# State matrices in column halves where the neighbours run in column halves, and an order of work grouped by the tiling of the TensorE array

## Chip, cores, metric

One core of one Trainium2 chip. The metric is the device time in microseconds of one execution. Several executions of each kernel were timed; one of each run was also profiled, and its span (first to last instruction) is about 2 us (1.7 to 2.3 in the record) shorter than its timed value. Some executions show a lower granted TensorE clock (down to 0.983 in the record), or are over 1.5% above the fastest of their kernel; the record calls them slow. Medians below are of all executions, ratios of fast ones alone. The experiments ran in four sittings, on chips 10, 14, 1 and 12, each beside the kernel before in the same rounds. In the profiles PE is TensorE, PEld its weight loads, DVE VectorE, ACT ScalarE, POOL GpSimd, SP SyncE; a "q" behind a name is the engine's instruction queue.

## The reference, cut to what matters

```python
# A: a diagonal state-space layer, 640 complex states, 2048 steps, 640 channels
Lam_bar = jnp.exp(dt * Lam)
h = Lam_bar[None, :] * h + Bu[:, t, :]                 # for t in range(2048)
y = 2.0 * jnp.einsum("blp,dp->bld", hseq, Cmat).real + x * Dskip
# B: shifted k times v, a long convolution over 2048 steps by FFT, times q
y = irfft(rfft(kv, 4096) * rfft(ssm_k, 4096))[:2048] + kv * ssm_D
out = jnp.concatenate([a, q * y], axis=-1)             # 2048 x 1280, bfloat16
```

## The kernel before

The kernel computes A by blocks: projections into the states, powers of the state matrices (`M[n]`, 128x128) that carry a state over n steps, and an output projection. B is a transform in two stages forward (s1, s2) and two back (i2, i1). All of it is one graph of 722 operations; a text, `ORDER`, gives the order of emission, the engine and the buffer slot of each. What matters here is how the matmuls lie in the array; the sizes are those that the profile prints for the weights, 128*128 for the whole array:

```python
# dn (L630): 128 rows x 64 columns, two halves of the columns side by side
nc.tensor.matmul(P[64 * ri:64 * ri + 64, b, :], lhsT=self.BT[:, k, ri, 64 * j:64 * j + 64], rhs=self.xT[...])
# m1 (L638): the whole array
for r, n in ((2, 1), (1, 2), (0, 3)):
    nc.tensor.matmul(self.P(pt)[:, 1, 256:512], lhsT=M[n][:, j, :],
                     rhs=self.hb[:, j, hf, 256 * r:256 * r + 256], start=False, stop=True, skip_group_check=True)
# d0 (L731): the whole array, 512 columns; d1 (L715), S (L659), jw and jv (L677): the whole array
nc.tensor.matmul(self.P(p2)[:, 0, :]..., lhsT=M[1][:, j, :], rhs=src, start=True, stop=True)
# py (L778, L782): output projection and skip term, the whole array
nc.tensor.matmul(P[:, part, 0:320], lhsT=hap(j), rhs=self.CT[:, j, c0:c0 + 320], start=(j == 0), stop=False)
# s1 (L881): 64x64.  s2 (L917): 128x64.  i2 (L973): 64x128.  i1 (L1009): 128x64.  ct (L758): 64x128
...
ORDER = """
...
x131 dn1_4_0 e1_2_0/D e1_1_0/A set_4_0/G hst0/S@2 set_8_0/D m1_2_0 e3_0_0/A x100 m1_1_0 ct@3 dn0_9_0@6 ...
"""
```

Every `e...` is a copy out of PSUM (L209 on ScalarE, L211 on VectorE).

## Time and profile before

| | before |
|---|---|
| timed, median of 4 (range) | 211.53 us (210.95 to 213.7) |
| span of the profiled execution (itself timed at 213.1) | 210.9 us |
| TensorE busy | 194.0 us, 92% |
| VectorE, ScalarE busy | 169.3, 148.1 us |
| waits of TensorE that the profile lists | 12.8 us, 5.1 of them before its first matmul |

A reader should not stop at "92% busy". The ends of matmuls are modelled, so time lost between two matmuls can lie under the busy row (ten L630 that start at 54.84 last 1.25 us by the profile, and the next matmul starts 1.18 us after 54.84); the starts in the order of time show it. The prediction below quotes those lines. Its 111 and 98 ns are the mean durations of weight loads, and its 3 to 4 ns the time between the starts of the two matmuls of a pair.

### The profile page before, as it was taken

How to read it: one execution, taken by the hardware profiler on the slowest of the kernel's cores; microseconds unless marked ns; L12 is line 12 of the kernel's file. 1: busy time of each engine (PE TensorE's matmuls, PEld its weight loads, DVE VectorE, ACT ScalarE, POOL GpSimd, SP SyncE). 2: the span in 40 equal slices, each digit the busy share in tenths (PEclk: the TensorE clock that was granted, in tenths of full speed). 3: DMA queues.
4: the chain of work that ended last, by engine and by line, in shares of the span. 5: the costliest groups of instructions: out<-in, count | busy, mean ns of one | idle time of the engine just before them, and what ended most of it. 6: DMA issues, size and time to landing. Idle time of an engine off the chain costs nothing.

```text
span 210.9 us, 8671 instructions
## 1 busy us (share of the span) xinstructions
PE 194.0 (92%) x3947; PEld 132.6 (63%) x3947; DVE 169.3 (80%) x262; ACT 148.1 (70%) x174; POOL 28.4 (13%) x39
## 2 busy tenths in 40 slices
PE   0899999899998999997899999999999998999772
...
DVE  7899999958999697888679889888798798775540
...
GB/s 170 286 140 166 168 179 193 203 188 175 161 235 172 246 233 221 119 160 164 244 136 3 31 168 229 131 36 135 209 125 33 117 220 133 37 184 187 193 137 131
DMA packets 103094, 33.72 MB, mean 160 GB/s; under 512 B 99538, under 2 KB 101330, under 8 KB 103058
## 3 DMA queue, kind: packets, MB, share of 16 engines
...
q10 hardware_dynamic: 30, 0.00, 0.0%
HBM read 9.19 MB, written 7.86 MB: 81 GB/s over the span
## 4 chain that ended last, share of the span: by engine, by line
PE 60%; DMA 18%; DVE 12%; issue 5%; ACT 4%; POOL 0%; POOLq 0%; ACTq 0%; DVEq 0%
PE ps L778 19%; DMA s<-kvd 8%; PE ps L630 8%; PE ps L881 8%; PE ps L917 7%; DMA kvd<-s 5%; DMA s<-s 5%; PE ps L731 4%; PE ps L973 3%; PE ps L1009 3%; DVE s L940 3%; PE ps L782 2%; PE ps L715 2%; PE ps L638 1%; PE ps L758 1%
## 5 line engine op out<-in xcount | busy, mean ns | idle before, releaser
L209 ACT CAST s<-ps 128x1024 bf16<-128x1024 f32 x90 | 88.1, 1017 | 26.4 <-PE ps L881 10.3
L630 PE MATMUL ps<-xT,BC 128*64 128x512 bf16 x400 | 49.2, 386 | 0.2 <-ACT s L209 0.2
L778 PE MATMUL ps<-BC,hb 128*128 128x320 bf16 x240 | 36.6, 300 | 0.0
L630 PEld LDWEIGHTS <-BC 128*64 128x64 bf16 x400 | 21.3, 111 | 17.6 <-issue 2.4
L778 PEld LDWEIGHTS <-hb 128*128 128x128 bf16 x240 | 21.9, 98 | 9.5
L881 PE MATMUL ps<-R,s 64*64 64x128 bf16 x1280 | 23.9, 218 | 3.7 <-DMA s<-kvd 2.0
L940 DVE TENSOR_TENSOR s<-s,s 128x2048 bf16<-128x2048 bf16 x20 | 24.5, 1223 | 2.2 <-ACT s L209 1.5
L881 PEld LDWEIGHTS <-s 64*64 64x64 bf16 x1280 | 18.9, 106 | 10.1 <-issue 5.4
L735 DVE TENSOR_TENSOR hb<-ps,hb 128x512 bf16<-128x512 f32 x30 | 19.5, 685 | 5.2 <-PE ps L731 5.2
L209 ACT CAST yo<-ps 128x640 bf16<-128x640 f32 x10 | 6.9, 691 | 22.1 <-PE ps L782 21.5
L917 PE MATMUL ps<-s,Wre 128*64 128x128 bf16 x320 | 21.5, 222 | 0.0
L917 PE MATMUL ps<-s,Wim 128*64 128x128 bf16 x320 | 21.0, 219 | 0.0
L917 PEld LDWEIGHTS <-Wre 128*64 128x64 bf16 x320 | 17.4, 109 | 3.5 <-issue 1.3
L856 DVE TENSOR_TENSOR s<-s,s 128x2048 bf16<-128x2048 bf16 x15 | 18.5, 1237 | 0.8 <-ACT s L848 0.5
L917 PEld LDWEIGHTS <-Wim 128*64 128x64 bf16 x320 | 17.9, 110 | 0.8
L1016 DVE TENSOR_TENSOR s<-ps,s 128x1024 bf16<-128x1024 f32 x10 | 12.0, 1216 | 7.1 <-PE ps L1009 4.6
L211 DVE CAST s<-ps 128x1024 bf16<-128x1024 f32 x10 | 12.2, 1222 | 4.2 <-PE ps L973 1.8
L940 DVE TENSOR_TENSOR s<-s 128x1024 bf16<-128x1024 bf16 x20 | 13.7, 687 | 0.3
L1009 PE MATMUL ps<-Ct,s 128*64 128x64 bf16 x640 | 11.8, 196 | 1.8 <-DMA s<-s 1.8
L1009 PEld LDWEIGHTS <-s 128*64 128x64 bf16 x640 | 10.9, 113 | 3.3 <-DMA s<-s 2.0
L850 DVE TENSOR_SCALAR s<-s,sk 128x2048 bf16<-128x2048 bf16 x15 | 12.0, 808 | 0.3
L778 PE MATMUL ps<-BC,Qb 128*128 128x320 bf16 x80 | 12.2, 300 | 0.0
...
## 6 DMA issues: line engine op xcount, KB each, us to landing
...
```

What stands on the lines that cost most here:

```text
L209: self.nc.scalar.copy(out=out, in_=in_)
L211: self.eng[e].tensor_copy(out=out, in_=in_)
L630: nc.tensor.matmul(P[64 * ri:64 * ri + 64, b, :], lhsT=self.BT[:, k, ri, 64 * j:64 * j + 64], rhs=self.xT[:, k, hf, 2 * b:2 * b + 2, :].re ...
L735: v.tensor_tensor(out=hv(r), in0=self.P(p2)[:, 0, :].rearrange("p (h m) -> p h m", h=2), in1=hv(r), op=ALU.add)
L778: nc.tensor.matmul(P[:, part, 0:320], lhsT=hap(j), rhs=self.CT[:, j, c0:c0 + 320], start=(j == 0), stop=False)
L850: v.tensor_scalar_mul(out=out, in0=k(j), scalar1=self.sk[:, G, j:j + 1])
L856: op(f"ca{j}{G}{h}", {"DVE": dve_tt(W_)}, lambda e, c=c, tt=tt: v.tensor_tensor(out=c(), in0=c(), in1=tt(), op=ALU.add), r=[f"tm{G}{h}"], ...
L881: nc.tensor.matmul(P[64 * ri:64 * ri + 64, r, 128 * b4:128 * b4 + 128], lhsT=d[64 * r:64 * r + 64, 4 * qd + b4, a0, :], rhs=self.R[64 * r: ...
L917: nc.tensor.matmul(P[64 * pi:64 * pi + 64, ri, 128 * k4:128 * k4 + 128], lhsT=W[:, kp, pi, :], rhs=A[:, kp + 16 * pi, :], start=True, stop ...
L940: v.tensor_tensor(out=o, in0=a, in1=b, op=op_)
L1009: nc.tensor.matmul(P[64 * ah:64 * ah + 64, b // 8, 64 * (b % 8):64 * (b % 8) + 64], lhsT=Z[:, 16 * h + b, 64 * ri:64 * ri + 64], rhs=self. ...
L1016: v.tensor_tensor(out=o, in0=self.P(pt)[:].rearrange("p s (b a c) -> p a (s b) c", b=8, a=16), in1=o, op=ALU.mult)
```

## The change

Intent: TensorE loses time each time the tiling of the array changes, 0.10 us on leaving a block in the trace of before (called a drain below; it is a name for the measured loss, what the array does in it is not shown). So a whole-array matmul with a state matrix is emitted as two matmuls with 64 columns each where its neighbour that cannot choose runs in column halves; and the order is a new one in which work of one tiling stands together.

```diff
+FREE = ("m1_", "d0", "d1_", "S", "jw", "jv")
...
+    def split(self):
+        pe = [o for o in self.order if o.eng == "PE"]
+        before = None
+        for i, o in enumerate(pe):
+            if o.name.startswith(FREE):
+                if before is None:
+                    before = next((self.halves(q) for q in pe[i:] if not q.name.startswith(FREE)), None) or False
+                o.split = before
+            else:
+                before = self.halves(o)
+
+    def halves(self, o):
+        return True if o.name.startswith(("dn", "s2", "i1")) else False if o.name.startswith(("py", "px")) else None
...
+    def mm(self, o, out, lhsT, rhs, **k):
+        if self.g.by_name[o].split:
+            for h in (slice(0, 64), slice(64, 128)):
+                self.nc.tensor.matmul(out[h], lhsT=lhsT[:, h], rhs=rhs, **k)
+        else:
+            self.nc.tensor.matmul(out, lhsT=lhsT, rhs=rhs, **k)
...
-                nc.tensor.matmul(self.P(pt)[:, 1, 256:512], lhsT=M[n][:, j, :], ...
+                self.mm(f"m1_{u}", self.P(pt)[:, 1, 256:512], lhsT=M[n][:, j, :], ...
...                                   (the same for d0, d1, S, jw, jv)
 ORDER = """
-... (722 words, the old order)
+... (722 words, a new order; some copies and loads move to another engine or slot)
 """
```

(Cut: the helper's bookkeeping, cost figures that only label operations, and both orders.)

More of the change, by code (lines that the diff above doesn't have):

```diff
@@ L37 @@
     __slots__ = ("idx", "name", "alts", "fn", "deps", "succ", "bufs", "dma", "due", "own_due", "start", "end", "eng",
-                 "takes", "lat", "turn", "port")
+                 "takes", "lat", "turn", "port", "split")
 class Graph:
@@ L52, in __init__ @@
         self.order = []
+        self.by_name = {}
     def buf(self, tag, name, n=2):
@@ L59, in op @@
         o.idx, o.name, o.alts, o.fn, o.dma, o.own_due, o.turn = len(self.ops), name, alts, fn, dma, due, turn
-        o.lat, o.port = 2.0 if turn else 1.2, port
+        o.lat, o.port, o.split = 2.0 if turn else 1.2, port, False
         o.deps, o.succ, o.takes = set(), [], []
@@ L82, in op @@
         self.ops.append(o)
+        self.by_name[name] = o
         return o
@@ L87, in place @@
         letter = {"P": "PE", "A": "ACT", "D": "DVE", "G": "POOL", "S": "SP"}
-        ops = {o.name: o for o in self.ops}
+        ops = self.by_name
         done = set()
@@ L101, in place @@
         assert len(done) == len(self.ops)
+        self.split()
         return self.order
+    def split(self):
[10 more added lines that the diff above has]
+        return True if o.name.startswith(("dn", "s2", "i1")) else False if o.name.startswith(("py", "px")) else None
 def mm_cost(n, count=1):
@@ L126 @@
 ORDER = """
-ld_lre Dm0 w0 xn0@0 scol pidx B00 consts zero w1 J0 E0 kz1/G@0 kz0/G@1 wi0@2 w2 J1 ci0@1 ld_lim ld_ldt wi1@3 xn1@2 px00@0 bc
-B01 px02@1 ex00/A nrow wm1 kz2/G@4 c4 ex02/A par@2 px04@3 p0 wm0 dtb x130 px12@0 E1 ex04/A B10 nrowf px10@1 ex12/A px14@4 p1
-nrho fi rn mk ph x110 ci1 dn0_0_0@6 Dm1/S trig dn0_1_0@2 ex10/D ld_sk/S B11 ws0@5 ex14/D dn0_2_0@0 rc ss dn0_4_0@4 set_1_0/D
-set_2_1/G k0 dn1_0_0 set_2_0/D ws1@6 set_3_0/G dn1_1_0 x120 dn1_2_0 e1_0_0/D set_1_1/G m1_0_0 x131 dn1_4_0 e1_2_0/D e1_1_0/A
@@ L131 @@
-set_4_0/G hst0/S@2 set_8_0/D m1_2_0 e3_0_0/A x100 m1_1_0 ct@3 dn0_9_0@6 e3_1_0/D set_12_1/G dn0_8_0@2 sk e1_4_0/D dn1_9_0 R
-set_12_0/G v0@5 dn1_8_0 e1_9_0/A set_3_1/D m1_4_0 e3_2_0/A dn1_3_0@0 e3_4_0/A cs200/D@3 x111 e1_8_0/A dtap0/D m1_9_0 cv300/D@6
-s1h03@4,4 x121 e3_9_0/A ca200 m1_8_0 e1h03/A s1h00@6 dn0_3_0 x101 cs100/D e1h00/A ca100 s1h02@4 k1 e3_8_0/A s1h01@6 e1h02/A
-dn0_7_0@2 cs000/D e1h01/A den dn1_7_0 hst1/S@2 ca000 e1_3_0/A s2h01@4,5 m1_3_0 e2h01/A cm00 dn1_0_1@6 e1_7_0/A set_4_1/D
@@ L135 @@
-s2h03@4 kvs0/S cn10@0 dn0_0_1 e3_3_0/A g e2h03/A s2h02@0 dn0_4_1@4 e2h02/A dtap1/G m1_7_0 set_G_1/D set_8_1/G s1h11@0,2
-e3_7_0/A s1h13@2 e1h11/A dn1_4_1 e1_0_1/D set_G_0/G e1h13/A m1_0_1 s1h12@0 cs210/D@1 e1_4_1/A s1h10@2 e3_0_1/A cv310/D@3
-kvl0/S@5 v1@6 e1h12/A dn0_1_1@6 ca210 e1h10/A m1_4_1 k2 s1k03@0,1 cs110/D dn1_1_1 kz3/D@2 e1k03/A ca110 s1k01@2 e3_4_1/A V
-e1_1_1/D s1k00@0 e1k01/A s1k02@4 cs010/D e1k00/A dn1_3_1@2 ca010 e1k02/A m1_1_1 cm10 s2h00@0 e3_1_1/A e2h00/A cv320/D@5
-s2k01@4,0 s2k00@6 dn0_3_1 e2k00/D e2k01/A cn11@3 e1_3_1/A pP00@1 s2k02@0,6 s2k03@4 dn1_2_1@6 e2k02/A pQ00 m1_3_1 e2k03/A
@@ L140 @@
-kvs1/S s2h11@0,4 cn00 dn0_2_1 pY00 e3_3_1/A e2h11/A s2h12@4 e1_2_1/D i200@2,1 e2h12/A dn0_8_1@0 pP01@0 e300/A ld_dsk/S s2h13@4
-pQ01 dn1_8_1 e2h13/A kvl1/S@3 i201@2 pY01 dn0_9_1@4 v2@1 e301/A cs220/D@6 m1_2_1 e1_8_1/A i203@2 ca220 dn1_9_1 e3_2_1/A e303/A
-cs120/D S0@6 k3 e1_9_1/A ca120 m1_8_1 eS0/A s1k11@2,5 cs020/D m1_9_1 e3_8_1/A s1k13@6 e1k11/A cn01 ca020 dn1_6_1@0 e1k13/A
-i202@2 e3_9_1/D cm20 s1k12@4 hst2/S@4 e302/A s1k10@6 dn0_6_1 e1k12/D kvs2/S e1k10/A jw0@2 s2h10@4 e1_6_1/A jsw0 dn0_7_1@6
@@ L144 @@
-zt0@2 e2h10/A jcw0 s2k12@2,6 Ct s2k10@4,0 kz4/G@3 jaw00 e2k12/A dn1_7_1 scan0 dtap2/G e2k10/A dn1_5_0@2 e1_7_1/A s2k13@4 diagD
-dn0_5_0 e2k13/A jcv0 m1_7_1 e1_5_0/A dn1_6_0@4 pP11@1 q0/S@5 k4 e3_7_1/A m1_6_1 pQ11 s2k11@6 e3_6_1/A m1_5_0 e2k11/A dn1_5_1@0
-pY11 e3_5_0/A s1h20@6,5 s1h22@2 pP10@6 e1h20/A dn0_6_0 pQ10 e1h22/A dn0_5_1 e1_6_0/A pY10 i100@6 e1_5_1/A m1_6_0 v3@0 ob00
-i212@2,1 e3_6_0/A m1_5_1 e312/A i213@4 e3_5_1/D jv0@6 kvl2/G@1 S5@0 e313/A jsv0 jav01 i210@2 eS5/A jav00 i211@6 e310/A jw5@4
@@ L148 @@
-jcw5 hst3/S@6 s1h23@0 jsw5 e311/A ct00@2 jaw50 i101@4 scan5 e1h23/A ct01@6 ect01/A s1k21@0,4 zt1@2 ect00/A ob01 jv5@6 e1k21/A
-s1k23@2 jsv5 d1_1@4 e1k23/A ct10@0 dtap3/G a1_1 s1k22@6 ect10/A jcv5 ct11@2 d1_3@5 jav50 e1k22/A s1h21@0 jav51 d1_0@4 ob0/S
-a1_3 ect11/A q1/S@4 d1_2@6 a1_0 d1_4@7 e1h21/A d1_7@5 a1_2 ct20@2 d1_5@4 a1_7 d00_2@6 ect20/A ct21@0 a1_4 d1_6@5 ect21/A
-ct30@2 a00_2 d1_8@7 ect30/A ct31@0 a1_6 d1_9@6 a1_5 ect31/A ct40@2 d00_1@5 a1_8 d00_4@4 ect40/A ct41@0 a1_9 d00_7@7 ect41/A
-s1k20@2 a00_7 d00_8@6 py0_32@0,0 e1k20/A a00_1 a00_4 cv330/A@5 a00_8 d00_6@7 d00_3@5 d00_0@4 d00_5@2 a00_3 py1_32 a00_6
@@ L153 @@
-cs230/A@1 a00_5 d00_9@3 i110@6 a00_0 ey_32/A a00_9 d01_1@2 i111@4 st_32/S ca230 py0_03@0,1 a01_1 cs130/A ob10 py1_03 ob11
-d01_3@3 s1h33@6,1 ey_03/A d01_4@2 ca130 d01_9@4 e1h33/A st_03/S py0_33@0,0 ob1/S a01_9 cs030/A s1h32@6 a01_3 py1_33 a01_4
-e1h32/A hst4/S@2 ca030 d01_6@5 d01_8@4 ey_33/A d01_7@3 a01_6 py0_02@6,1 cs240/A@1 st_33/S a01_7 cm30 s2h20@0,0 py1_02 e2h20/A
-cv340/D@4 kvs3/S a01_8 s2h21@2 ey_02/A d01_0@5 dtap4/D ca240 s2k20@0,0 e2h21/A st_02/S py0_00@6,0 cs140/D e2k20/A ca140
-s2k21@2 kvl3/S@5 d01_5@4 d02_4@0 e2k21/A py1_00 a01_0 a01_5 d01_2@1 cs040/D py0_31@2,1 ey_00/A a01_2 st_00/S pP20@3 s1h30@4
@@ L158 @@
-d02_7@1 s2h23@6 e1h30/A a02_7 py1_31 a02_4 e2h23/A pQ20 s2h22@4 ey_31/A d02_1@1 py0_12@6,0 pY20 e2h22/A st_31/S d02_8@0 a02_1
-v4@0 i221@2,3 d02_2@4 a02_8 d02_3@5 e321/A d02_9@1 py1_12 a02_2 a02_3 d02_0@0 a02_9 s1h31@2 ey_12/A a02_0 d02_6@1 s1k32@4,2
-e1h31/A st_12/S a02_6 q4/S@6 d02_5@0 s1k31@6 a02_5 e1k32/A s1k33@2 ca040 s2h31@0,5 e1k31/A py0_21@4,1 cm40 q2/S@1 e2h31/A
-s1k30@6 e1k33/D kvs4/S py1_21 e1k30/A s2k31@0,0 ey_21/D s2k23@2,5 e2k31/A s2k22@6 st_21/G e2k23/D i220@4 e2k22/A py0_20@0,0
@@ L162 @@
-e320/A pP21@3 s2h32@2 s2k32@6,4 pQ21 e2h32/A s1h43@4,4 py1_20 e2k32/A pY21 e1h43/A s2k33@2 ey_20/D s2h33@6 s1h41@4 e2k33/D
-st_20/S e2h33/A py0_22@0,1 e1h41/A pP31@5 s1h42@6 s2h30@2 pQ31 e1h42/A s1h40@4 py1_22 kvl4/S@2 pY31 e1h40/A e2h30/A i222@6
-q3/G@4 ey_22/D i223@4 e322/A s2k30@2 st_22/S s2h41@0,0 e2k30/D e323/A py0_13@6,0 e2h41/A zt2@1 pP30@3 s1k42@4,2 s1k41@2 pQ30
-e1k42/A s1k40@0 py1_13 e1k41/A pY30 e1k40/A s1k43@4 ey_13/D s2h42@2 e1k43/A s2h40@0 st_13/G e2h42/D i233@6,5 e2h40/A s2k41@4,0
@@ L166 @@
-s2k40@2 e2k41/D py0_30@0,1 e2k40/A e333/A pP40@2 i232@4 s2k43@2,5 e332/A s2k42@6 pQ40 py1_30 e2k42/A pY40 e2k43/A s2h43@4
-i230@6 ey_30/D e2h43/A i231@2 e330/D i241@0,3 st_30/S e331/A py0_23@4,0 pP41@0 e341/A zt3@2 i120@6 pQ41 i240@2 py1_23 pY41
-e340/A i243@0 ey_23/A i242@2 e343/D st_23/S i121@4 e342/A ob20 py0_10@0,1 zt4@4 ob21 py1_10 ob2/G i131@2 ey_10/A py0_11@6,0
-ob31 st_10/S i130@4 py1_11 ob30 ob3/G ey_11/D i141@0 st_11/S i140@2 ob41 py0_01@4,1 ob40 ob4/S py1_01 ey_01/A st_01/S
+ld_lre kz2/D@0 w0 xn0@0 scol pidx Dm0 B00 consts J0 w1 E0 kz1/G@1 ci0@1 w2 zero J1 c4 wi1@2 ld_lim ld_ldt xn1@2 wi0@3 bc
@@ new lines @@
+px00@0 B01 px02@1 wm1 nrow ex00/A ex02/A par@2 px04@3 p0 nrowf dtb Dm1/S wm0 B10 px10@0 ex04/A px12@1 E1 px14@2 p1 ex12/A nrho
+x121 fi mk rn ph ci1 ld_sk/S dn0_2_0@4 x130 ex10/D trig dn0_0_0@6 B11 ex14/D ws1@4 R dn1_2_0 rc ss dn1_1_0@0 set_3_0/D
+set_2_0/G dn1_0_0 e1_2_0/A dn1_4_0@2 set_1_0/D ws0@5 k0@6 kz0/G set_1_1/G x131 dn0_4_0 e1_0_0/D hst0/S@2 m1_2_0 x120 set_3_1/G
+dn0_1_0 e3_2_0/D e1_4_0/D m1_0_0 dn1_8_0@4 ct@3 set_2_1/G e3_0_0/D e1_1_0/D dn0_8_0 sk x101 cv300/D@4 dn1_9_0@6 set_4_1/D
+m1_1_0 dn0_9_0 cs200/D@3 v0@5 e1_8_0/A dtap0/D set_8_1/D m1_4_0 e3_1_0/A m1_8_0 e3_4_0/A ca200 s1h03@0,4 x100 e3_8_0/A s1h01@2
@@ new lines @@
+e1h03/A dn0_3_0@4 cs100/D x111 e1h01/A ca100 s1h00@0 x110 e1_9_0/A s1h02@2 cs000/D dn1_3_0 kz3/G@2 e1h00/A ca000 hst1/S@6
+m1_9_0 e1h02/A dn1_7_0@0 cm00 e1_3_0/A s2h02@2,5 den kvs0/S dn0_7_0 e3_9_0/A k1 e2h02/A set_12_0/D s2h03@6 m1_3_0 g e2h03/A
+dn0_4_1@2 e1_7_0/A s2h01@6 dn1_4_1 e2h01/A dtap1/D set_G_0/G set_8_0/D m1_7_0 e3_3_0/A kvl0/S@3 s1h10@6,0 e3_7_0/A k2 s1h12@4
+e1h10/A set_G_1/D dn0_0_1@0 set_12_1/G e1h12/A s1h11@6 set_4_0/D dn1_0_1 e1_4_1/A ld_dsk/G e1h11/A m1_4_1 cv310/D@5 s1h13@4
@@ new lines @@
+e3_4_1/A cs210/D@4 v1@6 s1k03@6,2 e1h13/A dn0_1_1@2 ca210 e1k03/A s1k00@4 cs110/D e1_0_1/A s1k02@6 V dn1_1_1 e1k00/D e1k02/A
+m1_0_1 ca110 e1_1_1/A s2h00@4 s1k01@6 e3_0_1/A cs010/D m1_1_1 e1k01/A dn1_3_1@0 cv320/D@3 e3_1_1/A ca010 s2k03@6,1 e2h00/A
+dn0_3_1 cm10 e2k03/A s2k01@2,4 s2k00@4 e2k01/A kvs1/S dn1_2_1@6 e2k00/D k3 e1_3_1/A s2k02@2 pP00@6 s2h11@4,1 e2k02/A dn0_2_1
+pQ00 e2h11/A m1_3_1 cn00@3 dn0_8_1@2 e3_3_1/A pP01@5 e1_2_1/A s2h12@4 s2h13@0 pY00 e2h12/A dn1_8_1 e2h13/A m1_2_1 pQ01
+kvl1/S@4 i200@4,4 e3_2_1/A i201@0 e300/A pY01 S0@6 v2@6 e301/A dn1_9_1@4 cs220/D@1 eS0/A ca220 i202@0 e1_8_1/A i203@6 cn10
@@ new lines @@
+dn0_9_1 cs120/D e302/A ca120 e303/A s1k10@0,2 m1_8_1 cs020/D e1_9_1/A zt0@5 dn1_6_1@6 e3_8_1/D e1k10/A ca020 m1_9_1 s1k11@2
+e3_9_1/A s1k13@0 cm20 e1k11/A s1k12@4 dn0_6_1 e1k13/A e1k12/D jw0@2 e1_6_1/A s2h10@0 q0/S@5 jsw0 dn0_7_1@4 cn11@0 e2h10/A Ct
+jcw0 jaw00 scan0 hst2/S@0 s2k13@2,1 s2k12@0 e2k13/A dn1_7_1 e2k12/A dn1_5_0@2 e1_7_1/A s2k11@0,4 pP11@6 cn01 dn0_5_0 e2k11/A
+pQ11 m1_7_1 s2k10@0 e3_7_1/A m1_6_1 e2k10/A pY11 dn1_6_0@4 e1_5_0/A i100@0 pP10@1 kvs2/S e3_6_1/A dn0_6_0 dtap2/G ob00 m1_5_0
@@ new lines @@
+s1h22@6,4 e3_5_0/A pQ10 e1_6_0/A s1h20@0 dn1_5_1@2 e1h22/A pY10 dn0_5_1 e1h20/A kz4/G@3 k4 diagD hst3/S@4 jv0@6 e1_5_1/A
+i213@0,2 jsv0 m1_6_0 e313/A m1_5_1 i211@6 e3_5_1/D e3_6_0/A i212@0 jcv0 e311/A i210@2 kvl2/S@6 jav00 S5@4 v3@1 jav01 e312/A
+e310/D d1_0@6 eS5/A ct00@0 a1_0 ct01@2 ect00/A jw5@4 jcw5 s1h23@6 ect01/A dtap3/D jsw5 ct10@0 e1h23/A ct11@2 jaw50 i101@4
+scan5 ect11/A ct20@6 ect10/A s1h21@2 ect20/A s1k23@0,1 q1/S@0 ob01 e1h21/A d1_2@6 d1_3@7 a1_2 jv5@4 ob0/S e1k23/A ct21@2 zt1@5
+jsv5 ect21/A ct30@0 jcv5 s1k21@4 jav51 ect30/A s1k22@2 jav50 d1_4@6 e1k21/A a1_3 d1_9@0 d1_5@1 a1_4 e1k22/A d1_7@7 a1_9 d1_6@6
@@ new lines @@
+ct31@4 a1_5 ct40@2 ect31/A d1_1@0 a1_6 d1_8@1 a1_7 ect40/A ct41@4 d00_6@6 a1_8 ect41/A d00_7@7 d00_0@2 a1_1 d00_5@3 cs230/A@5
+d00_2@1 d00_8@0 a00_5 py0_32@4,0 a00_6 a00_2 py1_32 a00_7 a00_8 s1k20@6 ey_32/A a00_0 d00_9@3 d00_4@1 e1k20/A st_32/S d00_3@0
+a00_9 d00_1@2 i111@4 a00_1 cv330/A@6 a00_3 i110@6 a00_4 s1h33@2,0 ca230 py0_03@0,1 e1h33/A ob11 cs130/A py1_03 ob10 py0_33@2,0
+ey_03/A ca130 st_03/S ob1/S py1_33 cs030/D ca030 d01_1@4 s1h32@6 ey_33/A a01_1 s1h30@0 st_33/S e1h32/A cm30 d01_9@5 hst4/S@2
@@ new lines @@
+d01_3@4 py0_02@2,1 cv340/A@5 cs240/D@1 kvs3/S a01_9 py1_02 e1h30/A ca240 d01_0@5 py0_00@6,0 ey_02/D cs140/A a01_0 st_02/S
+dtap4/G s2h20@0,3 a01_3 d01_8@5 s2k21@2,0 e2h20/A a01_8 d01_6@4 py1_00 kvl3/S@6 ca140 e2k21/A a01_6 s2k20@0 ey_00/A d01_5@5
+d01_2@4 e2k20/A d02_6@2 st_00/G a01_5 s2h21@6 d01_4@3 a02_6 d01_7@5 e2h21/A py0_31@0,1 a01_7 cs040/A a01_2 s1k33@6,2 a01_4
+s1k30@4 s1k32@2 pP20@3 e1k30/A py1_31 e1k32/A ca040 py0_12@4,0 e1k33/A pQ20 q4/S@1 ey_31/A py1_12 pY20 st_31/S d02_5@2 s2h23@6
@@ new lines @@
+v4@0 ey_12/A a02_5 d02_3@3 s2h22@0 e2h23/A a02_3 d02_1@2 d02_7@4 d02_2@5 a02_1 e2h22/A s1k31@6 st_12/S a02_2 d02_9@3 e1k31/A
+s1h31@0 a02_9 d02_4@2 a02_7 d02_8@5 e1h31/A s2k22@6,6 d02_0@3 a02_8 e2k22/A i220@0,5 a02_4 i221@4 a02_0 e320/A s2h33@6,4 cm40
+s2h30@2 py0_21@0,1 e2h30/A e2h33/D kvs4/S e321/A py1_21 s2k23@2 ey_21/A s2h32@6 e2k23/D st_21/S s1h40@4,1 e2h32/A s1h42@0
+kvl4/S@4 pP21@3 s2k31@2,0 e1h42/A py0_20@6,0 e2k31/D e1h40/A s2k32@0,5 pQ21 s2k33@4 e2k32/A s2h31@2 py1_20 pY21 e2k33/A pP31@6
@@ new lines @@
+py0_22@0,1 ey_20/A e2h31/A st_20/S pQ31 s1h41@4 s1k40@6,0 pY31 s1h43@2 e1k40/A py1_22 q2/S@2 e1h41/D e1h43/A s2k30@6 ey_22/D
+s2h41@2,3 e2k30/A i223@4 st_22/G e2h41/D s1k41@0 e323/A s1k42@6 pP30@5 py0_13@2,0 e1k42/A pQ30 e1k41/A py1_13 pY30 s1k43@4
+i222@6 ey_13/D e1k43/A i231@0,2 e322/D st_13/S i232@2 e331/A s2k40@4,4 e332/D s2k41@6 zt2@4 e2k40/A s2h42@0 e2h42/D e2k41/A
+s2h40@2 i230@4 e2h40/A i233@6 e330/D py0_30@0,1 e333/A pP40@0 s2h43@2 s2k42@4,3 pQ40 zt3@1 e2h43/A s2k43@6 py1_30 pY40 e2k42/A
@@ L170 @@
+e2k43/A py0_23@2,0 ey_30/A pP41@5 i121@4 pQ41 st_30/S q3/S@6 i240@6,0 i241@0 pY41 e340/A py1_23 e341/A i242@6 ey_23/A i243@0
+e342/A st_23/G i120@2 e343/D py0_10@6,1 ob20 zt4@5 ob21 i131@0 i130@2 ob31 py1_10 ob30 ob2/S py0_11@4,0 ey_10/D st_10/S ob3/S
+py1_11 i140@0 ey_11/A st_11/G i141@2 ob40 py0_01@6,1 ob41 py1_01 ob4/S ey_01/A st_01/S
 """
@@ L295, in f_par @@
                                  start=True, stop=True)
-        op("par", {"PE": 0.1}, f_par, r=["praw", "ident"], w=["par"], bufs=[self.par], due=-25)
+        op("par", {"PE": 0.17}, f_par, r=["praw", "ident"], w=["par"], bufs=[self.par], due=-25)
         def f_nrow():
@@ L580, in f @@
                                                  rhs=self.ident[:], start=True, stop=True, is_transpose=True)
-                op(f"px{b}{k}", {"PE": mm_cost(128, 4 * w)}, f, r=[f"xn{b}", "ident"], w=[f"px{b}{k}"], bufs=[pt, xa],
+                op(f"px{b}{k}", {"PE": 0.225 * w}, f, r=[f"xn{b}", "ident"], w=[f"px{b}{k}"], bufs=[pt, xa],
                    due=self.DUE["x0"] + 0.5 * k + 3.0 * b)
@@ L637, in f1 @@
             for r, n in ((2, 1), (1, 2), (0, 3)):
-                nc.tensor.matmul(self.P(pt)[:, 1, 256:512], lhsT=M[n][:, j, :], rhs=self.hb[:, j, hf, 256 * r:256 * r + 256],
+                self.mm(f"m1_{u}", self.P(pt)[:, 1, 256:512], lhsT=M[n][:, j, :], rhs=self.hb[:, j, hf, 256 * r:256 * r + 256],
                                  start=False, stop=True, skip_group_check=True)
-        op(f"m1_{u}", {"PE": mm_cost(256, 3)}, f1, r=[f"h_{u}", f"M_1_{h}", f"M_2_{h}", f"M_3_{h}"], w=[f"pu1_{u}"], bufs=[pt], due=due)
+        op(f"m1_{u}", {"PE": 0.335}, f1, r=[f"h_{u}", f"M_1_{h}", f"M_2_{h}", f"M_3_{h}"], w=[f"pu1_{u}"], bufs=[pt], due=due)
         self.evac(f"e3_{u}", 256, lambda: self.Qb[:, j, 1 + 2 * hf:3 + 2 * hf, :].rearrange("p q n -> p (q n)"),
@@ L658, in fS @@
                 for c, (lt, q) in enumerate(((self.ident, 4), (self.M[4][:, j, :], 3), (self.M[8][:, j, :], 2), (self.M[12][:, j, :], 1))):
-                    nc.tensor.matmul(P[:, 128 * i:128 * i + 128], lhsT=lt[:] if c == 0 else lt, rhs=self.Qb[:, j, q, :],
+                    self.mm(f"S{nm}", P[:, 128 * i:128 * i + 128], lhsT=lt[:] if c == 0 else lt, rhs=self.Qb[:, j, q, :],
                                      start=(c == 0), stop=(c == 3))
@@ L676, in fj @@
                     w = min(512, N - c)
-                    nc.tensor.matmul(P[:, c:c + w], lhsT=self.J[:], rhs=flat(src())[:, c:c + w], start=True, stop=True)
+                    self.mm(f"j{tag}{nm}", P[:, c:c + w], lhsT=self.J[:], rhs=flat(src())[:, c:c + w], start=True, stop=True)
             op(f"j{tag}{nm}", {"PE": mm_cost(N)}, fj, r=rkeys + ["J"], w=[f"pj{tag}{nm}"], bufs=[pt], due=due)
@@ L714, in f1 @@
             for n, w in ((4, 384), (8, 256), (12, 128)):
-                nc.tensor.matmul(P[:, 0, 384 - w:384], lhsT=M[n][:, j, :], rhs=rhs[:, 0:w], start=(n == 4), stop=(n == 12))
-        op(f"d1_{j}", {"PE": mm_cost(768)}, f1, r=[f"Q0_{j}", f"q_{j}", "Qz", f"M_4_{h}", f"M_8_{h}", f"M_12_{h}"], w=[f"pd{j}"],
+                self.mm(f"d1_{j}", P[:, 0, 384 - w:384], lhsT=M[n][:, j, :], rhs=rhs[:, 0:w], start=(n == 4), stop=(n == 12))
+        op(f"d1_{j}", {"PE": 0.33}, f1, r=[f"Q0_{j}", f"q_{j}", "Qz", f"M_4_{h}", f"M_8_{h}", f"M_12_{h}"], w=[f"pd{j}"],
            bufs=[pt], due=due)
@@ L730, in f3 @@
                 src = self.Qb[:, j, 0:4, :].rearrange("p (h q) n -> p h (q n)", h=2) if r == 0 else hv(r - 1)
-                nc.tensor.matmul(self.P(p2)[:, 0, :].rearrange("p (h m) -> p h m", h=2), lhsT=M[1][:, j, :], rhs=src, start=True, stop=True)
+                self.mm(f"d0{r}_{j}", self.P(p2)[:, 0, :].rearrange("p (h m) -> p h m", h=2), lhsT=M[1][:, j, :], rhs=src, start=True, stop=True)
             op(f"d0{r}_{j}", {"PE": mm_cost(512)}, f3, r=[f"f3_{j}", f"Q0_{j}"] if r == 0 else [f"f{r - 1}_{j}"], w=[f"pe{r}_{j}"], bufs=[p2], due=due)
```

12 lines of the change are left out of this document (6 added, 6 removed).

## The prediction

> **What bounds the kernel now.** I read the page first (engines, slices, chain), then who waits for whom, then TensorE's instructions in order of time, then busy time by stretches of 10 us.
>
> The page, with its parts on engines, slices and chain:
>
> ```profile
> PE 194.0 (92%) x3947; PEld 132.6 (63%) x3947; DVE 169.3 (80%) x262; ACT 148.1 (70%) x174; POOL 28.4 (13%) x39
> PE   0899999899998999997899999999999998999772
> DVE  7899999958999697888679889888798798775540
> PE 60%; DMA 18%; DVE 12%; issue 5%; ACT 4%; POOL 0%; POOLq 0%; ACTq 0%; DVEq 0%
> ```
>
> TensorE is busy in nearly every slice and holds 60% of the chain. VectorE is second at 80%.
>
> Who waits for whom, TensorE's lines alone (in total, times, longest):
>
> ```profile
> PE ps L579 <- DVE Jt L288: 5.1, 1, 5.1
> PE ps L881 <- DMA s<-kvd: 2.0, 3, 1.0
> PE ps L1009 <- DMA s<-s: 1.8, 1, 1.8
> PE ps L881 <- issue: 1.0, 1, 1.0
> ```
>
> After its first instruction it hardly waits. But "busy" hides one loss, which only the starts show. TensorE in order of time, 54 to 59 us (start, duration with the modelled end, what):
>
> ```profile
> 54.84 1.25 PE L630 MATMUL ps<-xT,BC 128*64 128x512 bf16 x10
> 56.02 0.50 PE L638 MATMUL ps<-hb,M 128*128 128x256 bf16 x3
> 56.45 0.25 PE L917 MATMUL ps<-s,Wre 128*64 128x128 bf16 x2
> 56.53 0.22 PE L917 MATMUL ps<-s,Wim 128*64 128x128 bf16 x2
> ...
> 56.92 1.25 PE L630 MATMUL ps<-xT,BC 128*64 128x512 bf16 x10
> 58.00 0.22 PE L917 MATMUL ps<-s,Wre 128*64 128x128 bf16 x2
> ...
> 58.40 0.22 PE L917 MATMUL ps<-s,Wim 128*64 128x128 bf16 x2
> 58.55 0.23 PE L973 MATMUL ps<-s,Vre 64*128 64x128 bf16 x2
> ```
>
> "128*64" is the shape of the weights: rows by columns of the array. From 56.92 to 58.00 ten L630 matmuls take 1.08 us up to the next start, where L917 follows in the same tiling. From 54.84 to 56.02 they take 1.18, where the full-array L638 follows. From 58.40 to 58.55 a pair of L917 takes 0.15 before L973, and 0.055 between pairs otherwise. **A change of tiling costs 0.10 us on leaving**, and the first weights afterwards come late: the second pair of L917 follows 0.08 us after the first (56.45, 56.53), not 0.055. Over all blocks the medians agree: last start to next start is 213 against 312 ns (L630), 52 against 152 (L917), 46 against 148 (L881), 109 against 203 (L638); on entry a column-tiled block loses 24 ns more, another 11 ns.
>
> [...]111 ns for 128x64 (L630), 98 ns for 128x128 (L778), so half of the weights takes as long as all. [...]3 to 4 ns within an L630 or L917 pair, and a pair of 512 columns repeats every 216 ns, just as a full-array L731 matmul. [...]the drains lie under the busy row of 92%.
>
> **The sum for TensorE before.** First matmul at 5.1 us, last block's start at 205.4, end of the span at 210.9. The blocks without change of tiling: L630 40 x 1.079 = 43.2; L778 with L782 31 x 1.50 = 46.5; L881 40 x 0.447 = 17.9; L917 40 x 0.446 = 17.8; L973 20 x 0.446 = 8.9; L1009 10 x 1.01 = 10.1; L638 20 x 0.327 = 6.5; L731 30 x 0.216 = 6.5; L715 10 x 0.327 = 3.3; the rest some 10. Sum about 170.8. The 167 changes of tiling take 18.9. What is left of the 200.4 is waiting, 10.6 us: 1.9 for the last transposed load, about 2 at the start, and a dozen gaps of 0.2 to 1.3.
>
> **The change, part by part.** The built program's order and the rule for splitting give the changes of tiling.
>
> Old order, whole matmuls: 167. New order, all still whole: 135. Old order with splitting: 135. **Both: 95**, so 72 fewer. The new order puts several L778/L782 blocks, L881 blocks and L731 steps beside their own kind. The splitting turns 18 of 20 L638 blocks, 18 of 30 L731 blocks, one L659 and two L677 blocks into pairs of halves.
>
> Removed: 72 x 0.099 on leaving = 7.1 us. On entry, column-tiled blocks go from 77 to 53, 24 x 0.024 = 0.6; others from 90 to 42, 48 x 0.011 = 0.5. Together **8.2 us**. Of the 72, some 47 lie in the first 120 us of TensorE's own work and the rest after it.
>
> Added: 96 matmuls and 96 weight loads (18 x 3 + 18 + 20 + 4). A pair of halves streams beside itself, 3 to 4 ns apart, so it lasts as one whole matmul; I put 1 ns a pair, 0.1 us. The loads add 96 x 0.11 = 10.6 us to a row that is busy 63% beside the stream: nothing on the path.
>
> Not gained: at the end, TensorE waits for the last transposed load (issued about 190.5, landed 200.9), while it does two L1009 blocks and four L778 blocks. Both orders do the same there, so the two drains saved in that stretch (0.2 us) only lengthen the wait.
>
> The moves between engines are small: VectorE loses copies of 0.95 us (3) and of 0.82 (2) and one scaling, and gains three net copies of 1.22 and two of 0.42 to 1.22; with two 1.12 us constant-matrix builds moved to it I count some 2.3 us more for VectorE, 1 more for ScalarE.
>
> Sum with unchanged waits: 210.9 - 8.2 + 0.1 + 0.2 = 203.0 us.
>
> **The rivals.** (1) **VectorE becomes the bound.** Busy time by stretches of 10 us (columns: PE, PEld, DVE, ACT, POOL):
>
> ```profile
> 50.00:60.00 10.00, 10.00 (x184) 6.56 (x183) 9.75 (x10) 9.17 (x12) 0.00 (x0) 1.00 1.17 175
> 60.00:70.00 10.00, 9.35 (x179) 5.83 (x177) 9.19 (x12) 7.61 (x11) 0.00 (x0) 1.00 1.17 228
> 110.00:120.00 10.00, 10.00 (x188) 7.25 (x186) 9.66 (x14) 7.32 (x5) 0.00 (x0) 1.00 0.06 18
> ```
>
> From 10 to 190 us VectorE works 152.8 of 180 us, 85%. In the new kernel it must do about 155.1 in some 172, 90%. The third column shows 9.2 to 9.75 in its fullest stretches, so 90% is possible but not easy. For: the stage from 50 to 110 us, where the convolution, the products and the scan feed each other, already keeps it full. Against: it waits mostly for TensorE (5.2 us for L731, 4.6 for L1009), which comes sooner now. If it held 87% only, the stretch would last 178 us and the span 209.
>
> (2) **Buffers.** Blocks of one kind in a row fill PSUM faster than ScalarE's copies (1.02 us each for 0.45 us of matmuls) empty it. I took TensorE's own time between the end of one use of a bank and the next, less the copy: less than 0.5 us is left in 14 of some 210 reuses of the old order, in 34 of the new. [...]Twenty tighter places at 0.1 to 0.2 us make 2 to 4 us.
>
> (3) **The halves cost more than I say**, or the drain stays. Against: L630 and L917 are of this form and follow each other without a gap. Then only the new order's 32 changes (3.6 us) would be gained: 207.
>
> **Range and chances.** I take 203.0 and add 2.5 us of new waits from (1) and (2), which overlap: 205.5 us. The timed runs are within 0.7 of the span and I leave it there. Low end: waits shrink a little, 201.5. High end: VectorE binds or the halves disappoint, 209.5. Two per cent faster is 207.3; I give that 0.75, within 2% 0.23, slower 0.02.
>
> **What would show it right or wrong.** Right: L638 and most of L731 stand as 128*64 in twice the number; ten L630 matmuls take 1.08 us up to the start of L638; the starts show no more than 95 gaps of 0.10; PEld busy rises to some 143 us; VectorE's share rises to about 84%. Wrong: a pair of halves of L638 repeating in clearly more than 0.11 us; gaps that stay at 0.10 between L630 and L638; TensorE's waits for ScalarE or VectorE grown by over 4 us, above all between 50 and 110 us; the last transposed load issued less than 5 us earlier than now.

## The result, and the profile after

Ratios are the mean time of one kernel's fast runs over that of the other's of the same rounds, so not quite the ratio of the medians quoted. Of the changed kernel's four, 205.31 is a slow one (clock 0.992).

| | before | changed |
|---|---|---|
| timed, median of 4 | 211.53 us | 203.66 us (202.26 to 205.31) |
| ratio, 95% interval | | 0.9588 (0.9492 to 0.9684) |
| span of the profiled execution | 210.9 | 200.5 |
| changes of tiling | 167 | 95 |

The lines of code moved: L630 is now L658, L778 and L782 are L806 and L810, L881 is L909, L917 is L945, L973 is L1001, L1009 is L1037, the copies L209 and L211 are L237 and L239. Matmuls with state matrices now come from the helper: L231 in halves, L233 whole.

The page of the changed kernel, the lines that were shown of before:

```profile
PE 185.7 (93%) x4043; PEld 136.3 (68%) x4043; DVE 168.1 (84%) x264; ACT 148.1 (74%) x175; POOL 20.6 (10%) x35
PE   0599999979999999699999999999999999999982
DVE  7899899876899999949988899788959999877540
PE 72%; DMA 14%; DVE 6%; ACT 3%; SPq 2%; issue 1%; POOL 0%; DVEq 0%; POOLq 0%; ACTq 0%
```

TensorE's busy time fell by 8.3 us although it has 96 matmuls more. Its share did not fall: the drains had been counted as busy.

TensorE in order of time, the same kind of place as in the prediction (start, duration, what):

```profile
55.42 1.27 PE L658 MATMUL ps<-xT,BC 128*64 128x512 bf16 x10
56.50 0.52 PE L231 MATMUL ps<-hb,M 128*64 128x256 bf16 x6
56.83 1.27 PE L658 MATMUL ps<-xT,BC 128*64 128x512 bf16 x10
57.91 0.25 PE L945 MATMUL ps<-s,Wre 128*64 128x128 bf16 x2
```

From 55.42 to 56.50 is 1.08 us, where it was 1.18 ahead of a whole L638. The six halves take 0.33 us to the next start, where the three whole matmuls took 0.43. The 0.10 is gone on both sides. A block of L731, one step of 512 columns in two halves, stands between L945 pairs without a gap (0.21 us):

```profile
125.19 0.22 PE L945 MATMUL ps<-s,Wim 128*64 128x128 bf16 x2
125.25 0.38 PE L231 MATMUL ps<-hb,M 128*64 128x512 bf16 x2
125.46 0.22 PE L945 MATMUL ps<-s,Wre 128*64 128x128 bf16 x2
```

Where the tiling still changes, the cost is as before: medians of this trace from the first start of a block to the next block are 1079 ns in one tiling and 1178 before a change for L658 (a single block), 447 and 549 for L909, 447 and 546 for L945, 1499 and 1593 for a projection block.

Who waits for whom, all that the profile lists for TensorE after the change:

```profile
PE ps L607 <- DMA s<-in_A_x_dram: 7.0, 2, 5.0
PE ps L909 <- POOL s L831: 1.8, 1, 1.8
PE ps L909 <- ACT s L237: 1.1, 1, 1.1
PE ps L1037 <- DMA s<-s: 0.7, 1, 0.7
PE ps L786 <- ACT s L237: 0.2, 1, 0.2
```

L607 is the transposes of x at the start. Waits were not removed so much as moved: in this trace the read-backs (`s<-kvd`) no longer hold TensorE, a filter load does (by way of GpSimd's L831). In the repeats r1 and r3 below the filter load costs 1.8 us again, and a read-back 0.5 and 1.4.

**An account that all traces can share.** For each trace I took the matmul starts, the blocks' times in one tiling (171.1 us together in every kernel), the counted changes at 0.097 us on leaving and 0.024 (column tilings) or 0.011 (others) on entry, and called the rest up to the last block "waits". The drains are thus a count times the medians of these traces, and waits are a remainder. The figures of the prediction (18.9 and 10.6) differ by rounding.

| trace | changes | drains | waits | span |
|---|---|---|---|---|
| before; again | 167 | 19.0 | 10.3; 10.6 | 210.9; 211.3 |
| changed; again; third | 95 | 10.9 | 8.1; 11.2; 9.6 | 200.5; 203.6; 202.0 |
| new order, whole (e1) | 135 | 15.4 | 12.2 | 208.9 |
| old order, split (e2) | 135 | 15.4 | 8.9 | 206.0 |
| all state matmuls in halves (e4) | 100 | 11.6 | 8.8 | 202.4 |
| projection in halves too (e3) | 76 | 9.0 | 14.8 | 205.2 |
| the same but the tail (e5) | 81 | 9.5 | 11.9 | 203.0 |
| one load earlier (v1) | 95 | 10.9 | 11.0 | 203.2 |
| loads reordered (v3) | 95 | 10.9 | 7.5 | 199.8 |
| v3 and nine projection blocks (v4) | 84 | 9.7 | 7.9 | 198.9 |

### The profile page after: what moved, and what is told of

Same layout as the page of the kernel before. It is cut to its first block, busy times and chain, and to the rows that moved or that the text cites. A ratio compares the mean times of both kernels' runs of the same rounds, so it can differ in the third digit from the quotient of the medians.

```text
span 200.5 us, 8859 instructions
## 1 busy us (share of the span) xinstructions
PE 185.7 (93%) x4043; PEld 136.3 (68%) x4043; DVE 168.1 (84%) x264; ACT 148.1 (74%) x175; POOL 20.6 (10%) x35
## 4 chain that ended last, share of the span: by engine, by line
PE 72%; DMA 14%; DVE 6%; ACT 3%; SPq 2%; issue 1%; POOL 0%; DVEq 0%; POOLq 0%; ACTq 0%
PE ps L806 20%; PE ps L658 17%; PE ps L909 9%; PE ps L945 8%; PE ps L231 4%; DMA s<-s 4%; PE ps L1001 4%; DMA s<-in_B_v_dram 4%; PE ps L233 4%; PE ps L1037 3%; DMA s<-in_A_x_dram 3%; DMA s<-in_B_ssm_k_dram 3%; DVE s L239 2%; PE ps L810 2%; ACT s L237 2%
## 5 line engine op out<-in xcount | busy, mean ns | idle before, releaser
L237 ACT CAST s<-ps 128x1024 bf16<-128x1024 f32 x86 | 84.1, 1018 | 16.9 <-PE ps L945 6.4
L658 PE MATMUL ps<-xT,BC 128*64 128x512 bf16 x400 | 49.1, 383 | 0.1
L806 PE MATMUL ps<-BC,hb 128*128 128x320 bf16 x240 | 36.4, 300 | 0.0
L658 PEld LDWEIGHTS <-BC 128*64 128x64 bf16 x400 | 22.3, 110 | 15.1 <-issue 0.9
L806 PEld LDWEIGHTS <-hb 128*128 128x128 bf16 x240 | 21.9, 98 | 8.7 <-issue 0.3
L909 PE MATMUL ps<-R,s 64*64 64x128 bf16 x1280 | 22.5, 218 | 2.9 <-POOL s L831 1.8
L237 ACT CAST yo<-ps 128x640 bf16<-128x640 f32 x12 | 8.4, 698 | 22.7 <-PE ps L810 18.5
L909 PEld LDWEIGHTS <-s 64*64 64x64 bf16 x1280 | 18.7, 107 | 8.1 <-issue 3.7
L239 DVE CAST s<-ps 128x1024 bf16<-128x1024 f32 x14 | 17.0, 1220 | 8.3 <-PE ps L909 2.7
L945 PE MATMUL ps<-s,Wre 128*64 128x128 bf16 x320 | 21.4, 221 | 0.0
L945 PE MATMUL ps<-s,Wim 128*64 128x128 bf16 x320 | 21.2, 219 | 0.0
L945 PEld LDWEIGHTS <-Wre 128*64 128x64 bf16 x320 | 18.2, 110 | 2.5 <-issue 0.5
L945 PEld LDWEIGHTS <-Wim 128*64 128x64 bf16 x320 | 18.1, 110 | 1.1
L237 ACT CAST hb<-ps 128x768 bf16<-128x768 f32 x17 | 13.7, 808 | 1.1 <-PE ps L658 1.1
L231 PE MATMUL ps<-hb,M 128*64 128x256 bf16 (+1 forms) x136 | 13.3, 296 | 0.0
L1037 PE MATMUL ps<-Ct,s 128*64 128x64 bf16 x640 | 11.6, 196 | 0.8 <-DMA s<-s 0.7
L1037 PEld LDWEIGHTS <-s 128*64 128x64 bf16 x640 | 11.1, 113 | 1.9 <-DMA s<-s 0.9
```

The source lines that it names most:

```text
L231: self.nc.tensor.matmul(out[h], lhsT=lhsT[:, h], rhs=rhs, **k)
L237: self.nc.scalar.copy(out=out, in_=in_)
L239: self.eng[e].tensor_copy(out=out, in_=in_)
L909: nc.tensor.matmul(P[64 * ri:64 * ri + 64, r, 128 * b4:128 * b4 + 128], lhsT=d[64 * r:64 * r + 64, 4 * qd + b4, a0, :], rhs=self.R[64 * r: ...
L945: nc.tensor.matmul(P[64 * pi:64 * pi + 64, ri, 128 * k4:128 * k4 + 128], lhsT=W[:, kp, pi, :], rhs=A[:, kp + 16 * pi, :], start=True, stop ...
L1037: nc.tensor.matmul(P[64 * ah:64 * ah + 64, b // 8, 64 * (b % 8):64 * (b % 8) + 64], lhsT=Z[:, 16 * h + b, 64 * ri:64 * ri + 64], rhs=self. ...
```

## The experiments

Theory: the gain is the drains, 0.113 us for each change of tiling that goes (18.9 us over 167). Rivals: the order alone gains by its waits; the halves cost something of their own.

**e1, the new order with whole matmuls.**

```diff
-        self.split()
         return self.order
```

> The new order with every matmul left whole: 135 changes of tiling instead of 95. Drain theory (each change costs about 0.113 us, as the trace of before gave it): 40 x 0.113 = 4.5 us more than the changed kernel, so about 208, ratio to the kernel before 0.984. Rival 'the order alone': the new order wins by its waits, the splitting is worth nothing: about 203.7, ratio 0.963.

Measured: 209.19 us, ratio 0.9857 (0.979 to 0.9924). The drain theory had 0.984, the rival 0.963. The new order alone is worth 1.4% and the splitting the rest. (Here and in e2 the interval excludes 1 but includes 0.98, so that by the record's 2% the verdict is "unclear".) Its trace has 40 changes more than the changed kernel (4.5 us) and more waits as well (12.2 us), among them 5.5 us that the profile calls "issue"; see below. The traced execution was the longest of its four.

**e2, the old order with the splitting rule.** The text `ORDER` of the kernel before in the changed kernel, nothing else.

> The old order with the splitting rule: 135 changes instead of 167. Drain theory: 32 x 0.113 = 3.6 us less than the kernel before, about 207.9, ratio 0.983, and gaps of 0.10 us between L630-like blocks and the m1 blocks gone. Rival 'the order alone': 211.5, ratio 1.0. Rival 'the splitting alone': about 203.7, ratio 0.963.

Measured: 208.91 us, ratio 0.9846 (0.9769 to 0.9923), where the drain theory had 0.983. The two parts are worth 32 changes each alone and 72 together: grouping puts more of the matmuls that can choose beside column-tiled neighbours, and the splitting joins groups that the order alone leaves apart.

**e4, all state matmuls in halves whatever the neighbour.**

```diff
-                o.split = before
+                o.split = True
```

> The new order with all of the state matmuls in halves whatever their neighbours, the projection whole: 100 changes instead of 95. Drain theory: 0.6 us more than the changed kernel, about 204.2, ratio 0.966, hardly to be told from it by the time; the trace should show the pairs of halves repeating at 110 ns for 256 columns and 216 for 512. Rival 'halves cost': 72 more matmuls cost visibly more than that, 1 us or above.

Measured: 204.47 us, ratio 0.9606 (0.9524 to 0.9688), not to be told from the changed kernel's 0.9588 to 0.9606. 72 more halves cost nothing that shows. The interval, 0.8% either way, would not exclude the rival's 1 us; the trace speaks against it, where the halves of 256 columns take 0.327 us for the six and a step of 512 columns 0.216, as the whole ones do.

**e3, the output projection in halves too.** In addition to e4:

```diff
-                    nc.tensor.matmul(P[:, part, 0:320], lhsT=hap(j), ...
+                    self.mm(f"py{part}_{r}{i}", P[:, part, 0:320], lhsT=hap(j), ...
...                                   (the same for the diagD matmuls; o.split = True for "py")
```

> The new order with all of the state matmuls and also the output projection (the 128x320 matmuls and those with diagD) in halves: 76 changes instead of 95, 4043 + 72 + 416 = 4531 matmuls and as many weight loads. Drain theory with free halves: 19 x 0.113 = 2.1 us less than the changed kernel, about 201.5, ratio 0.953. Rival 'halves cost': a projection pair of 320 columns repeats slower than 136 ns because its two weight loads (2 x 110 ns) no longer hide; then 205 or more, ratio 0.97 or above, and the PEld row near 180 us.

Measured: 207.05 us, ratio 0.9721 (0.965 to 0.9791). The drain theory had 0.953, so it missed by 2%; the rival had the time about right, for a reason that the trace denies. A projection block in halves in e3, then a whole one in the changed kernel (start, duration, what):

```profile
146.29 1.52 PE L232 MATMUL ps<-BC,hb 128*64 128x320 bf16 x20
147.65 0.31 PE L232 MATMUL ps<-diagD,xT 128*64 128x128 bf16 x6
```

```profile
121.47 1.52 PE L806 MATMUL ps<-BC,hb 128*128 128x320 bf16 x10
122.83 0.30 PE L810 MATMUL ps<-diagD,xT 128*128 128x64 bf16 x3
```

Twenty halves take 1.36 us, ten whole ones 1.36 us. PEld is at 143.6 us, not 180. The loss is elsewhere, in the last 25 us of e3:

```profile
183.25 1.14 PE L1038 MATMUL ps<-Ct,s 128*64 128x64 bf16 x61 [0.58 <-issue]
...
187.26 1.55 PE L1038 MATMUL ps<-Ct,s 128*64 128x64 bf16 x87 [0.70 <-issue]
...
192.91 0.57 PE L232 MATMUL ps<-BC,hb 128*64 128x320 bf16 x5 [1.51 <-issue]
...
197.73 0.76 PE L1038 MATMUL ps<-Ct,s 128*64 128x64 bf16 x37 [1.19 <-issue]
```

"[1.51 <-issue]" is idle time for which the profile knows no releaser, here in the middle of blocks that have all their data. These four stand after the 4058th, 4186th, 4314th and 4442nd matmul: 128 apart, exactly. The page counts one weight load for each matmul, so 128 matmuls make 256 instructions, and the trace's packets of the instruction queue land within some 0.6 us of the last start before each of the gaps. Across all fourteen traces that I read, such waits named "issue" of 0.7 us and more inside blocks fall 88 to 93 matmuls after a multiple of 128.

**e5, the same with the last projection blocks whole.**

```diff
-                o.split = o.name.startswith("py")
+                o.split = o.name.startswith("py") and o.name[-2:] not in ("10", "11", "01")
```

> The all-halves kernel, but the last three blocks pairs of the output projection whole: 81 changes of tiling, 4453 matmuls. In the all-halves trace four gaps of 0.8 to 1.8 us (4.9 us) stand in the last 25 us, each ending 1.0 to 1.7 us after a packet of the instruction queue began to land late. Theory 'instructions come too late where small matmuls are densest': these gaps go (the tail has as few instructions as in the changed kernel), ratio about 0.957 or lower, 202.5. Rival 'halving the projection is slow in itself' or plain chance: about 0.972 again, 206 to 207.

Measured: 204.18 us, ratio 0.9629 (0.9564 to 0.9693). The gaps of the tail went from four with 4.8 us to two with 1.7 us, and three fifths of e3's loss against the expected 0.957 came back. That speaks for late instructions where many small matmuls stand together, but not all the way: 0.957 was expected, and e1, with the fewest instructions of all, had 5.5 us of such waits.

The traces say more than these two times. The queue q8 of kind "instruction" moves packets of 16384 bytes, one for each 128 matmuls (31 in the changed kernel). Over the fourteen traces, 39 of the 40 waits named "issue" of more than 0.15 us stand 88 to 93 matmuls after a multiple of 128, and each lasts until 1.25 to 1.73 us after the packet of that place (the nth for the nth place) has landed. At the 383 such places passed with no wait over 0.15 us, the packet had landed at least 1.29 us before. So these stops go with packets that land late; what makes one packet come late and another in time stays open.

**r1, the changed kernel again; r2, the kernel before again; r3, the changed kernel a third time.** No edit.

> The changed kernel once more, with a second trace and more timed runs, beside the next three on the same chip. Drain theory: ratio 0.959 again, 95 gaps of tiling, about 10.9 us of them, and waits of 8 to 10 us in the trace. If the first trace owed its low waits to luck (no gap without a releaser in it, while the kernel before had three), this one shows one or two such gaps of about 1 us and a span near 201.9.

> The kernel before once more, for a second trace. Drain theory: again 167 gaps of tiling, about 19 us of them. Waits: 10 us or so; if the three gaps of about 1 us that no releaser explains (in the blocks of lines 881, 973 and 782) stand at other instructions or in other number, they are chance of the execution and not of the kernel's order.

> The changed kernel a third time, to stand beside the next one on the same chip: ratio 0.959 to 0.960; 95 gaps, waits 8 to 11 us.

Measured: r1 203.57 us, ratio 0.9603 (0.9545 to 0.966); r3 203.55, 0.9606 (0.957 to 0.9643). The result repeats. r2, one execution, 213.58 (its state unknown). The waits of the three traces of the changed kernel are 8.1, 11.2 and 9.6 us, of the two of before 10.3 and 10.6: the first trace's low figure was luck, and on average the waits changed by less than 1 us. It was not the luck that r1's expectation named: in r1 the gaps without a releaser are 0.9 us in all, none over 0.4, and in r3 the profile lists none. The spread comes from several places, among them the start (L607: 7.0, 8.0 and 7.4 us) and the read-backs. In r2 two of the three unexplained gaps stand after the same matmuls as in the first trace (the 1756th and the 3931st), the third does not, and another came. So they are bound to places in the instruction stream, with chance on top.

**v1, one load earlier.** The changed kernel, one word of `ORDER` moved:

```diff
-... dn0_7_1@4 cn11@0 e2h10/A Ct jcw0 jaw00 scan0 hst2/S@0 s2k13@2,1 ...
+... dn0_7_1@4 hst2/S@0 cn11@0 e2h10/A Ct jcw0 jaw00 scan0 s2k13@2,1 ...
```

> The changed kernel with one load (the third group's filter) issued ahead of a transposed load instead of behind it. In three traces of the new order TensorE waits 1.8 us at one place for this load. Theory: the wait goes, the drains stay at 95: 1.2 to 1.9 us less than the changed kernel, ratio 0.951. Rival: another wait takes its place (the second chain of that stage, or the transposed loads delayed by 0.5 us), ratio 0.957 to 0.959.

Measured: 206.18 us, ratio 0.9714 (0.9643 to 0.9786): slower than the changed kernel, beyond what the rival had. (Three of its five fast runs carry a clock of 0.989 to 0.992; the two at full clock took 205.03 and 205.31, still 1.6 us above the 203.57 of r1.) The wait of 1.8 us is gone; in its place stand, in the waits of TensorE and in VectorE's order of time:

```profile
PE ps L1037 <- DVE cw L709: 3.0, 1, 3.0
```

```profile
95.73 0.23 DVE L831 TENSOR_TENSOR s<-s,Dm 128x16 bf16<-128x16 bf16 x1 [3.20 <-DMA s<-in_B_ssm_k_dram]
```

VectorE now waits for the next group's filter load and holds up the matrix product behind it. The queue of SyncE shows why. There the load follows a transposed load, which waits for a store (`kvd<-s`) to land:

```profile
83.31 0.53 SPq L888 DMA_DIRECT2D kvd<-s  x1
88.34 1.97 SPq L844 DMA_TRANSPOSE s<-in_B_k_dram  x1
90.41 0.52 SPq L828 DMA_DIRECT2D s<-in_B_ssm_k_dram  x1
```

In the changed kernel the last two stood at 86.29 and 88.16. The transposed load waited 4.4 us for that store here and 2.7 there; why the store landed later is not shown.

**v2, v1 with nine projection blocks in halves.** The choice of halves is the one with the fewest changes of tiling, at a price for each added matmul, the tail left whole; a fixed list of names takes the place of the rule.

> The load earlier, and the choice of halves made by the fewest changes of tiling with a price on added matmuls; nine blocks of the output projection outside the tail are halved too: 84 changes instead of 95, 213 added matmuls instead of 96. Drain theory: 11 x 0.113 = 1.2 us less than the kernel with the load earlier alone, ratio about 0.945. Rival 'instructions come too late': the 117 added pairs of instructions bring one or two gaps of 1 us and eat it, ratio 0.951 or above.

Measured: 205.33 us (200.62 to 207.06), but five of its six runs were in the slow state (granted clock 0.990 to 0.992), so there is no ratio and I draw nothing from it.

**v3, both loads out of the way.** v1, and the transposed load behind the read-back:

```diff
-... kz4/G@3 k4 diagD hst3/S@4 jv0@6 ... i210@2 kvl2/S@6 jav00 ...
+... kz4/G@3 diagD hst3/S@4 jv0@6 ... i210@2 kvl2/S@6 k4 jav00 ...
```

> The kernel with the third group's filter load earlier, and now the fifth group's transposed load moved behind the third group's read-back, so that the fourth group's filter load no longer queues behind it (that queue made a new wait of 3.0 us in the kernel with the one load moved). Theory: both the 1.8 us wait and the 3.0 us wait are gone: 1.2 to 1.9 us less than the changed kernel, ratio 0.951 to 0.954. Rival: yet another load becomes late in this stage, ratio 0.96 or above.

Measured: 202.16 us (200.68 to 203.2), ratio 0.9542 (0.9504 to 0.958), beside 203.55 and 0.9606 of the changed kernel on the same chip: 0.7% faster, as expected but at the low end, with the two intervals overlapping a little. Both waits are gone from its trace; all that TensorE waits for there:

```profile
PE ps L607 <- DMA s<-in_A_x_dram: 6.5, 2, 5.0
PE ps L945 <- issue: 1.0, 1, 1.0
PE ps L909 <- DMA s<-kvd: 0.3, 1, 0.3
PE ps L786 <- ACT s L237: 0.2, 1, 0.2
PE ps L1001 <- DVE s L968: 0.2, 1, 0.2
PE ps L1037 <- DMA s<-s: 0.2, 1, 0.2
```

**v4, v3 with v2's list of halves.**

> The kernel with the loads reordered (ratio 0.954), and nine of the 32 blocks of the output projection in halves too: 84 changes of tiling instead of 95, 4160 matmuls instead of 4043. Drain theory: 11 x 0.113 = 1.2 us less, ratio 0.9485, about 201.0. Rival 'instructions come too late where they are denser': no gain, ratio 0.954 or above, with gaps of about 1 us after the instruction queue's packets in the trace.

Measured: 200.96 us, the lowest median of the study, but ratio 0.955 with an interval of 0.9457 to 0.9644: four fast runs lie between 200.06 and 201.13, one at 203.05, and the runs of before beside it spread from 208.9 to 212.5. The record's verdict is "unclear"; five of the eleven runs of before are left out as slow there, four of them at full clock, since one run of 208.88 sets the mark. Whether it beats v3 is unclear. It beats the kernel before: the whole interval lies below 0.98.

## Why the prediction was right, point by point

**Changes of tiling, 167 to 95.** Right: counted from the built order, and the blocks of the new trace show the tilings as named. L231 has 108 matmuls of 256 columns (18 blocks of six), as the prediction had it.

**0.099 us on leaving, 0.024 or 0.011 on entry, 8.2 us in sum.** Right. With the medians of both traces the drains fell by 8.1 us. e1 and e2 show it from both sides: 40 changes put back make 2.7% (0.9857 against 0.9588, some 5.7 us, of which 4.5 are drains by the account; the rest lies within the intervals), 32 taken from the old order make 1.5%.

**Halves last as long as whole matmuls.** Right: 0.11 us for 256 columns (0.33 for the six of L231), 0.21 for 512, 1.36 for a projection block. e4 shows no cost in the time.

**96 weight loads add 10.6 us to PEld.** Wrong in size: 132.6 became 136.3. The row counts time in which any load runs, and the two loads of a pair overlap: in the first trace of the changed kernel the 192 loads of halves last 21.1 us added up and cover 9.4. Nothing hung on it. Nor on the durations of the loads: half of the weights in 111 ns against all in 98 is what the trace of before shows, and no run here shows why half takes no less time.

**The tail keeps its wait.** Partly: the last transposed load was issued 7.8 us earlier (182.7 instead of 190.5) and TensorE's wait for it shrank from 1.8 to 0.7 us in the first trace. It did not grow by the 0.2 us that I set aside.

**VectorE gets 2.3 us more work.** Wrong: 169.3 became 168.1. The two constant builds added 1.2 us instead of 2.2, since their mean fell from 1119 to 969 ns, and the scalings got shorter too (808 to 752 ns). The share of 84% came out as said.

**"I add 2.5 us of new waits from (1) and (2)".** This is the term that was mis-sized. In three traces the waits are 8.1, 11.2 and 9.6 us against 10.3 and 10.6: on average 0.8 less. VectorE did not bind: in the first trace it was busy 9.3 to 9.7 us in several stretches of 10 us, and in all three TensorE waited for it for at most 0.4 us after the start-up. The 34 reuses of PSUM with less than 0.5 us to spare cost some: waits for ScalarE's copies within the work are 1.3 us in the first trace, 0.6 and 0.2 in the others, against 0.2 before. So twenty places at "0.1 to 0.2 us each", a guess of mine that no trace had given, were a few times too much, as far as the profile lists waits: most of the spare time, though below 0.5, was enough.

**"The timed runs are within 0.7 of the span and I leave it there."** This was wrong too, and hid the first error. The profiled execution of before (span 210.9) was timed at 213.1, a long one among its like though in the fast state; another run of before, timed at 211.7, has a span of 209.4. Subtracting from the timed median instead, 211.5 - 8.2 + 0.3 = 203.6, which is what was measured (203.66). That it fits to a tenth is luck: the interval of the ratio is 2 us either way, and the changed kernel's waits differ by 3 us between traces. The prediction of 205.5 is this plus the 2.5 us of waits that did not come, less 0.6 for the mixed scales.

## What to carry to other kernels

Read the starts of the matmuls, not their busy row: a loss of 0.1 us at each change of tiling hid in a row that was "92% busy". Where operations can run in either tiling, let them take the tiling of their neighbours, and group the rest; the two together saved more changes (72) than the sum of each alone (32 and 32), and halving itself cost nothing that these traces show (0.33 us for three matmuls of 256 columns, whole or in halves). Before moving a load, look at what queues behind it: v1 removed a wait of 1.8 us and made one of 3.0, with SyncE issuing the next filter load at 90.41 us, behind a transposed load of 88.34.

## What these traces show of the array and of the instruction packets

- A change of tiling costs 0.097 us on leaving a block (0.093 to 0.103 for each of the twelve ordered pairs of 128x128, 128x64, 64x128 and 64x64, so any two of them count as different), and 0.024 us (into 64-column tilings) or 0.011 us (into others) more before the second group of matmuls.
- A full 128-column matmul ran as two halves at no cost that shows: 0.33 us for three of 256 columns either way (L638 before, L231 after).
- The two matmuls of a pair mostly start 3 to 4 ns apart (162 of some 200 pairs of L630 in the trace of before, with 19 at 25 ns and 15 together). In some blocks of the changed kernel the halves alternate at 31 and 78 ns, or start together, at the same sum of 109 ns a pair.
- TensorE stopped for up to 2 us at some of the places 128 matmuls apart: not over 0.4 us in the three traces of the changed kernel, 4.8 us together in the last 25 us of e3; each stop ended 1.25 to 1.73 us after its packet had landed.
